# Strassen's seven block products in a float32 attention and mixture-of-experts kernel, ordered by a list scheduler at build time

## The chip, the cores and the metric

The kernel runs on one core of a Trainium2 chip. The core has a matrix engine (TensorE, "PE" in the profile, with its weight loads shown apart as "PEld"), a vector engine (VectorE, "DVE"), a scalar engine (ScalarE, "ACT"), GpSimd ("POOL") and SyncE ("SP"), whose queue issues all of this kernel's DMA transfers. Each engine runs its own instructions in order and waits on semaphores for the others. The metric is the device time of one execution in microseconds (us); less is better.

## What is computed

Inputs are q, k and v (8 batches, 8 heads, 576 tokens, 64 dims), a gain g_norm (64), the probabilities of four experts for each of the 4608 tokens, and the experts' weights w1 (4 x 512 x 1024) and w2 (4 x 1024 x 512). All is float32.

```python
kv = np.einsum('bhsd,bhse->bhde', k, v)
out = np.einsum('bhsd,bhde->bhse', q, kv)
rms = np.sqrt(np.mean(out * out, axis=-1, keepdims=True) + 1e-06)
x = (out / rms * g_norm)            # then (B,H,S,D) -> (B*S, H*D) = (4608, 512)
p = domain_probs / (domain_probs.sum(-1, keepdims=True) + 1e-09)
for e in range(E):
    h = np.maximum(x @ w1[e], 0.0)
    out += p[:, e:e + 1] * (h @ w2[e])
```

Every token goes through all four experts, so the two matrix products of the experts, 4608 x 512 x 1024 and 4608 x 1024 x 512 for each of four, are most of the arithmetic.

## The kernel before

Tokens go through the experts in nine chunks of 512. Chunk b < 8 holds the first 512 tokens of batch b, the ninth the 64 tokens that remain of every batch. All weights stay in SBUF, loaded once (`load_w1` and `load_w2`, L102 to L114). The loops run over chunks outermost, then experts, then eight slices of 128 hidden units (the list `slots`, L296).

`up` (L227, matmul L232) makes one slice of hidden units for the 512 tokens of a chunk: four matmuls, each with a weight block of 128 x 128 and 512 columns of x, added up in one PSUM bank; then ACT takes the bank through relu into SBUF (L237). `down` (L240, matmul L246) multiplies each of the chunk's four token blocks with the 512 columns of w2 for that slice, one matmul for each block; the four sums stay in four PSUM banks over the eight slices. After the eighth, `merge` (L253) takes each bank, times the token's probability for this expert, into an accumulator in SBUF on DVE (L257 and L259), and after the fourth expert `store` (L266) writes it out.

The attention of a batch consists of pieces (`attention`, L211): `key_values` makes k.T @ v for two heads (L151), `turn_q` transposes a block of queries (L170, copied on DVE at L172), `attend` multiplies (L181), squares on ACT (L186), sums on DVE (L188), takes the power on GpSimd (L189 and L193), and scales on DVE (L194); `turn_x` transposes the result (L207) and ACT writes it, times g, to the chunk's x (L209). Each batch has four blocks of 128 tokens and a remainder of 64.

The order of every engine is the order in which the code is written (`tc.manual_schedule`, L276). Batch 0's attention comes first and by itself. Then the slots follow: `up` of a slot, `down` of the slot before, and one piece of the next batch's attention after some of them (L308). SP's queue holds, in order, the loads of batch 0, the first expert's weights, g, the probabilities (L277 to L283), the next batches' loads and the stores.

Of the kernel before, what the change touches and what calls it, by code (L numbers as in the profile page):

```python
# [10 lines left out]
ALU = mybir.AluOpType  # L11
# [4 lines left out]

@with_exitstack
def kernel(
# [27 lines left out]
    KC = DM // P  # L46
    FCH = F // P
    NCH = B + 1
    KR = 6
    KP = S // KR  # L50
    EPS = 1e-6
    assert H * D == DM == NT and D == 64 and P == 128 and KC == NPAIR
# [3 lines left out]
    wpool = ctx.enter_context(tc.tile_pool(name="wpool", bufs=1))  # L56
    inpool = ctx.enter_context(tc.tile_pool(name="inpool", bufs=1))
    apool = ctx.enter_context(tc.tile_pool(name="apool", bufs=2))
    xpool = ctx.enter_context(tc.tile_pool(name="xpool", bufs=2))
    hpool = ctx.enter_context(tc.tile_pool(name="hpool", bufs=3))  # L60
    opool = ctx.enter_context(tc.tile_pool(name="opool", bufs=1))
    psum_a = ctx.enter_context(tc.tile_pool(name="psum_a", bufs=2, space=bass.MemoryType.PSUM))
    psum_h = ctx.enter_context(tc.tile_pool(name="psum_h", bufs=2, space=bass.MemoryType.PSUM))
    psum_o = ctx.enter_context(tc.tile_pool(name="psum_o", bufs=1, space=bass.MemoryType.PSUM))
# [4 lines left out]
    x_rem = const.tile([P, KC, NT], F32, name="x_rem")  # L69
    kv_bd = [const.tile([P, NPAIR, P], F32, name=f"kv_bd{i}") for i in range(2)]  # L70
    NBLK = NCH * NR
# [3 lines left out]
    w1_sb = [wpool.tile([P, KC, F], F32, name=f"w1_{e}") for e in range(E)]  # L75
    w2_sb = [wpool.tile([P, FCH, DM], F32, name=f"w2_{e}") for e in range(E)]

# [1 line left out]
    keys, values, queries, queries_rem = {}, {}, {}, {}  # L79

    def load_kv(b):
        for hp in range(NPAIR):
            hs = slice(2 * hp, 2 * hp + 2)
            for kept, src, tag in ((keys, k, "k"), (values, v, "v")):
                t = inpool.tile([KP, 2, KR, D], F32, tag=tag, bufs=2, name=f"{tag}{b}_{hp}")
                nc.sync.dma_start(
                    out=t[:].rearrange("p h j d -> p h (j d)"),
                    in_=src[b, hs].rearrange("h (p j) d -> p h (j d)", j=KR),
                )
                kept[b, hp] = t  # L90

    def load_q(b):
        t = inpool.tile([P, NR, H, D], F32, tag="q", name=f"q{b}")
        src = q[b, :, 0:NT, :].rearrange("h (p r) d -> p r h d", r=NR)
        for r in range(NR):
            nc.sync.dma_start(out=t[:, r], in_=src[:, r])  # L96
        queries[b] = t
        t = inpool.tile([REM, H, D], F32, tag="qr", name=f"qr{b}")
        nc.sync.dma_start(out=t[:], in_=q[b, :, NT:S, :].rearrange("h p d -> p h d"))  # L99
        queries_rem[b] = t  # L100

    def load_w1(e):  # L102
        n = 2 if e == 0 else 1
        for i in range(n):
            fs = slice(i * F // n, (i + 1) * F // n)
            nc.sync.dma_start(
                out=w1_sb[e][:, :, fs],
                in_=moe_w1[e][:, fs].rearrange("(kc p) f -> p kc f", p=P),
            )

    def load_w2(e):
        nc.sync.dma_start(
            out=w2_sb[e][:], in_=moe_w2[e].rearrange("(fc p) d -> p fc d", p=P)
        )  # L114

    def load_probs():
        by_batch = moe_domain_probs.rearrange("(b s) e -> s b e", s=S)
        nc.sync.dma_start(
            out=p_all[:, 0:B * NR, :].rearrange("p (b r) e -> p b (r e)", r=NR),
            in_=by_batch[0:NT].rearrange("(p r) b e -> p b (r e)", r=NR),  # L120
        )
        for bb in range(2):
            nc.sync.dma_start(
                out=p_all[bb * REM:(bb + 1) * REM, B * NR:NBLK, :],
                in_=by_batch[NT:S, bb::2, :],
            )

    def norm_probs():
        nc.vector.reduce_sum(out=tot[:], in_=p_all[:], axis=AX.X)
        nc.vector.tensor_scalar_add(out=tot[:], in0=tot[:], scalar1=1e-9)  # L130
        nc.vector.reciprocal(out=inv[:], in_=tot[:])
        nc.vector.tensor_tensor(
            out=p_all[:], in0=p_all[:],
            in1=inv[:].unsqueeze(2).to_broadcast([P, NBLK, E]), op=ALU.mult,
        )

# [1 line left out]
    kv_ps, xT, qT, x_tok = {}, {}, {}, {}  # L138

    def bank(name):  # L140
        return psum_a.tile([P, NT], F32, tag="a", name=name)

    def key_values(b, hp):
        """k.T @ v of two heads; after the last pair, all heads' as diagonal blocks."""
        if hp == 0:
            kv_ps[b] = bank(f"kv{b}")
        ps = kv_ps[b][:, 0:NPAIR * D].rearrange("p (a d) -> p a d", d=D)
        kt, vt = keys.pop((b, hp)), values.pop((b, hp))
        for r in range(2):
            for j in range(KR):  # L150
                nc.tensor.matmul(  # L151
                    ps[r * D:(r + 1) * D, hp, :], lhsT=kt[:, r, j, :], rhs=vt[:, r, j, :],
                    start=(j == 0), stop=(j == KR - 1),
                )
        if hp == NPAIR - 1:
            for r in range(2):
                rows = slice(r * D, (r + 1) * D)
                nc.vector.tensor_copy(out=kv_bd[b % 2][rows, :, rows], in_=ps[rows])  # L158

    def rows_of(r):  # L160
        return P if r < NR else REM

    def turn_q(b, r):
        """Queries of block r (the remainder for r == NR) with head dims on partitions."""
        n = rows_of(r)
        ps = bank(f"qT_ps{b}_{r}")[:, 0:NPAIR * n].rearrange("p (a t) -> p a t", t=n)
        for hp in range(NPAIR):
            hs = slice(2 * hp, 2 * hp + 2)
            src = queries[b][:, r, hs, :] if r < NR else queries_rem[b][:, hs, :]
            nc.tensor.transpose(ps[:, hp, :], src, ident[:n, :n])  # L170
        t = apool.tile([P, NPAIR, P], F32, tag="qT", name=f"qT{b}_{r}")
        nc.vector.tensor_copy(out=t[:, :, 0:n], in_=ps)  # L172
        qT[b, r] = t

    def attend(b, r):
        """q @ (k.T @ v) of the block, each head's row over its root mean square."""
        n = rows_of(r)
        raw = bank(f"raw{b}_{r}")
        t = qT.pop((b, r))
        for hp in range(NPAIR):  # L180
            nc.tensor.matmul(  # L181
                raw[0:n, hp * P:(hp + 1) * P], lhsT=t[:, hp, 0:n], rhs=kv_bd[b % 2][:, hp, :],
            )
        x = apool.tile([P, H, D], F32, tag="x", name=f"x{b}_{r}")
        rawh = raw[0:n, :].rearrange("p (h d) -> p h d", d=D)
        nc.scalar.activation(out=x[0:n], in_=rawh, func=ACT.Square)  # L186
        ss = apool.tile([P, H], F32, tag="ss", name=f"ss{b}_{r}")
        nc.vector.reduce_sum(out=ss[0:n], in_=x[0:n], axis=AX.X)  # L188
        nc.gpsimd.tensor_scalar(  # L189
            out=ss[0:n], in0=ss[0:n], scalar1=1.0 / D, scalar2=EPS, op0=ALU.mult, op1=ALU.add,  # L190
        )
        rt = apool.tile([P, H], F32, tag="rt", name=f"rt{b}_{r}")
        nc.gpsimd.tensor_tensor(out=rt[0:n], in0=ss[0:n], in1=mhalf[0:n], op=ALU.pow)  # L193
        nc.vector.tensor_tensor(  # L194
            out=x[0:n], in0=rawh, in1=rt[0:n].unsqueeze(2).to_broadcast([n, H, D]), op=ALU.mult,
        )
        x_tok[b, r] = x

    def turn_x(b, r):
        """The block with model dims on partitions, by g_norm."""  # L200
        n = rows_of(r)
        if r == 0:
            xT[b] = xpool.tile([P, KC, NT], F32, tag="xT", name=f"xT{b}")
        x = x_tok.pop((b, r))[0:n].rearrange("p h d -> p (h d)")
        ps = bank(f"xT_ps{b}_{r}")[:, 0:KC * n].rearrange("p (c t) -> p c t", t=n)
        for kc in range(KC):
            nc.tensor.transpose(ps[:, kc, :], x[:, kc * P:(kc + 1) * P], ident[:n, :n])  # L207
# [131 lines left out]
```

## Time and profile before

| What | Before |
|---|---|
| Time, median of 3 runs (lowest to highest) | 2158.01 us (2157.3 to 2158.16) |
| Span of the profiled execution | 2155.6 us |
| DMA, from and to DRAM | 45.16 MB read, 9.44 MB written |
| Mean granted TensorE clock over the span | 0.999 of full speed |

The span runs from the first to the last instruction of one profiled execution; the time has some work around it that the span leaves out. "Busy" is the time in which an engine executed instructions. A group of the profile shows line, engine, operation, output and inputs by their names in the program, shape and count, then busy time and the mean of one in ns, then the engine's idle time just before these instructions and what ended it. A float32 matmul leaves two records. The mean of one matmul record is the time from its start to its end, and these overlap from one to the next; the pace of the engine is read from the distance between starts.

### The profile page before, as it was taken

The page shows a single profiled execution, that of the slowest core. Times are in us where ns is not written, and L with a number is a line of the kernel's source. Part 1 is how long each engine was busy: PE and PEld are TensorE (multiplying, and loading weights), DVE is VectorE, ACT ScalarE, POOL GpSimd, SP SyncE. Part 2 cuts the span into 40 slices and gives each one's busy share as a digit, 9 for nine tenths or more (in the row PEclk, how much of TensorE's full clock was granted, in tenths as well). Part 3 has the DMA queues.
Part 4 walks back from the last instruction along what each step waited for, and adds up shares of the span by engine and source line. Part 5 has one row for each costly group of instructions (what it writes and reads, how often), then busy time and mean ns, then how long its engine had stood idle before and what let it go on. Part 6 is the DMA issues. An engine that isn't in the chain of part 4 may idle for free.

```text
span 2155.6 us, 13617 instructions
## 1 busy us (share of the span) xinstructions
PE 2118.0 (98%) x6016; PEld 990.4 (46%) x6016; DVE 197.1 (9%) x287; ACT 222.8 (10%) x369; POOL 73.9 (3%) x86
## 2 busy tenths in 40 slices
PE   4999999999999999999999999999999999999998
PEld 4444444444444444444444444444444444444443
DVE  1011000110011001110010001100111000000000
ACT  1011100110011000110011001110011000000000
POOL 1001000100000000000010000000000000000000
PEclk9999999999999999999999999999999999999999
DMA  6180003000300003000300020000200000000000
GB/s 167 30 270 0 0 0 86 0 0 0 82 5 0 0 12 75 0 0 0 86 0 0 0 71 15 0 1 5 60 0 1 20 0 0 0 20 0 0 0 20
DMA packets 64666, 55.47 MB, mean 26 GB/s; under 512 B 41056, under 2 KB 53344, under 8 KB 64608
## 3 DMA queue, kind: packets, MB, share of 16 engines
q1 hardware_dynamic: 64608, 54.61, 9.4%
q8 instruction: 47, 0.77, 0.2%
q14 instruction: 11, 0.09, 0.0%
HBM read 45.16 MB, written 9.44 MB: 25 GB/s over the span
## 4 chain that ended last, share of the span: by engine, by line
PE 98%; DMA 1%; SPq 0%; POOL 0%; DVE 0%; ACT 0%; issue 0%; ACTq 0%
PE h_ps L232 46%; PE o L246 46%; PE kv L151 2%; PE raw L181 2%; PE xT_ps L207 1%; PE qT_ps L170 1%; DMA gcol<-in_g_norm_dram 1%; POOL rt L193 0%; SPq L96 0%; DMA v<-in_v_dram 0%; DVE x L194 0%; DVE ss L188 0%; ACT x L186 0%; SPq L282 0%; SPq L99 0%
## 5 line engine op out<-in xcount | busy, mean ns | idle before, releaser
L246 PE MATMUL o<-w,h 128*128 128x512 f32 x2304 | 1035.6, 592 | 0.0
L232 PE MATMUL h_ps<-xT,w 128*128 128x512 f32 x2048 | 928.0, 596 | 0.0
L246 PEld LDWEIGHTS o<-w,h 128*128 128x128 f32 x2304 | 437.8, 190 | 551.0 <-issue 551.0
L232 PEld LDWEIGHTS h_ps<-xT,w 128*128 128x128 f32 x2048 | 379.3, 190 | 431.1 <-issue 428.2
L237 ACT ACTIVATE h<-h_ps 128x512 f32<-128x512 f32 x288 | 172.0, 597 | 1626.4 <-PE h_ps L232 1626.4
L259 DVE SCALAR_TENSOR_TENSOR acc<-o,p_all,acc 128x512 f32<-128x512 f32 x108 | 81.1, 751 | 808.1 <-PE o L246 799.4
L232 PE MATMUL h_ps<-x_rem,w 128*128 128x512 f32 x256 | 115.1, 592 | 0.0
L232 PEld LDWEIGHTS h_ps<-x_rem,w 128*128 128x128 f32 x256 | 48.6, 190 | 61.2 <-issue 61.2
L193 POOL TENSOR_TENSOR rt<-ss,mhalf 128x8 f32<-128x8 f32 (+1 forms) x40 | 65.4, 1635 | 3.3
L188 DVE TENSOR_REDUCE ss<-x 128x8 f32<-128x512 f32 (+1 forms) x40 | 27.4, 684 | 399.6 <-ACT x L186 399.6
L189 POOL TENSOR_SCALAR ss<-ss 128x8 f32<-128x8 f32 (+1 forms) x40 | 7.8, 196 | 1569.6 <-DVE ss L188 1569.6
L151 PEld LDWEIGHTS kv<-v,k 96*64 96x64 f32 x768 | 45.3, 148 | 28.7 <-issue 28.7
L151 PE MATMUL kv<-v,k 96*64 96x64 f32 x768 | 49.6, 237 | 7.3 <-DMA v<-in_v_dram 7.3
L181 PEld LDWEIGHTS raw<-kv_bd,qT 128*128 128x128 f32 (+1 forms) x320 | 44.2, 197 | 20.2 <-issue 19.0
L181 PE MATMUL raw<-kv_bd,qT 128*128 128x128 f32 (+1 forms) x320 | 46.9, 294 | 0.8 <-DVE qT L172 0.8
L158 DVE COPY kv_bd<-kv 64x256 f32<-64x256 f32 x16 | 6.8, 422 | 394.6 <-PE kv L151 394.5
L207 PE MATMUL xT_ps<-ident,x 128*128 128x128 f32 (+1 forms) x160 | 25.1, 283 | 17.1 <-DVE x L194 17.1
L186 ACT ACTIVATE x<-raw 128x512 f32<-128x512 f32 (+1 forms) x40 | 23.8, 596 | 151.2 <-PE raw L181 151.2
L257 DVE TENSOR_SCALAR acc<-o,p_all 128x512 f32<-128x512 f32 x36 | 27.0, 751 | 131.6 <-PE o L246 128.6
L172 DVE COPY qT<-qT_ps 128x512 f32<-128x512 f32 (+1 forms) x40 | 25.5, 637 | 137.0 <-PE qT_ps L170 137.0
L207 PEld LDWEIGHTS xT_ps<-ident,x 128*128 128x128 f32 (+1 forms) x160 | 19.6, 150 | 39.0 <-issue 19.3
L194 DVE TENSOR_TENSOR x<-raw,rt 128x512 f32<-128x512 f32 (+1 forms) x40 | 27.6, 690 | 81.4 <-POOL rt L193 81.4
(19 smaller groups left out, 75.1 us busy)
## 6 DMA issues: line engine op xcount, KB each, us to landing
w<-in_moe_w_dram SPq DMA_DIRECT2D x7, 2048.0 KB, 18.4
k<-in_k_dram SPq DMA_DIRECT2D x32, 288.0 KB, 3.4
v<-in_v_dram SPq DMA_DIRECT2D x32, 288.0 KB, 4.0
q<-in_q_dram SPq DMA_DIRECT2D x32, 256.0 KB, 5.3
out_dram<-acc SPq DMA_DIRECT2D x32, 256.0 KB, 4.4
w<-in_moe_w_dram SPq DMA_DIRECT2D x2, 1024.0 KB, 7.9
qr<-in_q_dram SPq DMA_DIRECT2D x8, 128.0 KB, 4.7
out_dram<-acc SPq DMA_DIRECT2D x8, 128.0 KB, 2.3
```

The costliest lines, as they stand in the source:

```text
L151: nc.tensor.matmul(ps[r * D:(r + 1) * D, hp, :], lhsT=kt[:, r, j, :], rhs=vt[:, r, j, :], start=(j == 0), stop=(j == KR - 1),)
L172: nc.vector.tensor_copy(out=t[:, :, 0:n], in_=ps)
L181: nc.tensor.matmul(raw[0:n, hp * P:(hp + 1) * P], lhsT=t[:, hp, 0:n], rhs=kv_bd[b % 2][:, hp, :],)
L188: nc.vector.reduce_sum(out=ss[0:n], in_=x[0:n], axis=AX.X)
L193: nc.gpsimd.tensor_tensor(out=rt[0:n], in0=ss[0:n], in1=mhalf[0:n], op=ALU.pow)
L194: nc.vector.tensor_tensor(out=x[0:n], in0=rawh, in1=rt[0:n].unsqueeze(2).to_broadcast([n, H, D]), op=ALU.mult,)
L207: nc.tensor.transpose(ps[:, kc, :], x[:, kc * P:(kc + 1) * P], ident[:n, :n])
L232: nc.tensor.matmul(ps[:], lhsT=w1_sb[e][:, kc, fc * P:(fc + 1) * P], rhs=src[:, kc, :], start=(kc == 0), stop=(kc == KC - 1),)
L237: nc.scalar.activation(out=h[:], in_=ps[:], func=ACT.Relu)
L246: nc.tensor.matmul(o_ps[r][:], lhsT=h[:, r * P:(r + 1) * P], rhs=w2_sb[e][:, fc, :], start=(fc == 0), stop=(fc == FCH - 1),)
L257: nc.vector.tensor_scalar_mul(out=acc[r][:], in0=o_ps[r][:], scalar1=prob)
L259: nc.vector.scalar_tensor_tensor(out=acc[r][:], in0=o_ps[r][:], scalar=prob, in1=acc[r][:], op0=ALU.mult, op1=ALU.add,)
```

## The change

The matrix products of the experts are divided into blocks of halves in each of the three dimensions, and each product of two 2 x 2 block matrices is made with seven block products and additions (Strassen's scheme in Winograd's form) in place of eight. `up` and `down` do this each for itself: one step s is one expert on one chunk of 512 tokens, 36 steps in all, with the experts outermost now.

For that, sums and differences of blocks are needed. Of each expert's w1 and w2, four blocks are loaded and four more formed (`weights_1`, `weights_2`); of each chunk's x, four are formed (`x_forms`). As the experts are outermost, each chunk's x comes back for every expert: all seven blocks are written to DRAM when they are first made, and read from there for experts 1 to 3 (`x_again`). In the same way a chunk's partial output is written to DRAM after experts 0 to 2 and read back before the next.

In `up`, the products go in the order 1, 2, 6, 5, 7, 4, 3, each for two halves i of the columns. A product is four float32 matmuls with 256 columns. Products 1, 6, 7 and 4 add up in one PSUM bank, 5 and 3 in another that product 2 has used; between them ACT copies the bank, or DVE adds a copy to it and ACT takes the relu. From the four blocks of h that result, four more are formed on DVE or GpSimd. `down` works the same way for two halves t of the tokens; each time that a bank holds a term of the output, DVE merges its 256 columns, times the probability, into the output block.

```diff
+    def up(s, e, views):
...
+        for j, m in enumerate(ORDER):
+            for i in range(2):
...
+                if m == 1:
+                    banks[i, 1] = Buf("ub", f"u1_{n}")
+                elif m in (2, 5):
+                    banks[i, 2] = Buf("ub", f"u2_{n}")
+                ps = banks[i, 1 if m in (1, 6, 7, 4) else 2]
+
+                def product(eng, m=m, i=i, ps=ps):
+                    for u in range(2):
+                        cols = slice((2 * i + u) * P, (2 * i + u + 1) * P)
+                        for kt in range(2):
+                            nc.tensor.matmul(
+                                ps.ap[:, u * HN:(u + 1) * HN],
+                                lhsT=two(w1f[e][m].ap[:])[:, kt, cols], rhs=views[m][1]()[:, kt, :],
+                                start=(m in (1, 2, 5) and u == 0 and kt == 0), stop=(kt == 1),
+                                skip_group_check=True,
+                            )
...
+                if m in (1, 6, 7):
...
+                if m == 2:
+                    total(unit(1), ps, banks[i, -1])
+                elif m == 7:
+                    total(unit(4), banks[i, 2], banks[i, -7])
+                elif m == 4:
+                    relu(unit(2), ps, key - 0.4)
+                elif m == 3:
+                    total(unit(21), ps, banks[i, -6])
...
+                    form(5, 21, 4, ALU.add)
+                    form(7, 1, 21, ALU.subtract)
+                    form(6, 5, 1, ALU.subtract)
+                    form(3, 2, 6, ALU.subtract)
...
+    def down(s, e, c):
...
+        for t in range(2):
+            banks = {}
+            for j, m in enumerate(ORDER):
+                key = base + (7 * t + j + 0.5) / 14
+                kind = "ab" if e and t else "db"
...
+                def product(eng, m=m, t=t, ps=ps):
+                    for kt in range(4):
+                        src = h[m, kt // 2].ap[:].rearrange("p (u t) -> p u t", u=2)
+                        nc.tensor.matmul(
+                            ps.ap[:, 0:HN], lhsT=src[:, kt % 2, t * P:(t + 1) * P],
+                            rhs=w2f[e][m].ap[:, kt * HN:(kt + 1) * HN],
+                            start=(m in (1, 2, 5) and kt == 0), stop=(kt == 3),
+                            skip_group_check=True,
+                        )
...
+                if m in (1, 2):
+                    merge(key, ps, t, 0)
+                elif m in (6, 3):
+                    merge(key, ps, t, 1)
+                elif m in (5, 7):
+                    merge(key, ps, 2 + t, 1)
+                elif m == 4:
+                    merge(key, ps, 2 + t, 0)
```

SBUF and PSUM are divided into numbered slots: 20 "big" tiles of 1024 columns (blocks of weights, x of expert 0's chunks), 46 "small" ones of 512 (h, x, sums, attention), and eight PSUM banks: four for `up` ("ub"), two for `down` ("db") and two ("ab") for the attention, which `down` uses too for experts 1 to 3.

```diff
+    BANKS = {"ub": 4, "db": 2, "ab": 2}
+    SLOTS = {"big": 20, "small": 46, "kv": 6, "kvbd": 8, "ss": 4, "rt": 4, **BANKS}
...
+    def either(n):
+        return {"DVE": 0.17 + 0.00108 * n, "POOL": 0.1 + 0.0025 * n}
```

No engine's order is written by hand any more. Every operation is added to a plan with a key (its due time, in steps), an assumed duration on each engine that can do it, and what it reads and writes. Down products of step s have keys between s + 1 and s + 2, those of the up products of step s + 1, so that both kinds share PE. The planner (`Plan.layout`) goes through time with these assumed durations: whenever an engine is free, it starts the first operation in order of keys whose inputs and slots are ready by then, looking ahead of the earliest one that is left by at most `REACH` steps (0.7 on PE, 0.9 on DVE, ACT and GpSimd, 1.0 on SP). An operation marked `either` goes to DVE or GpSimd, whichever is free first. The order that results is written out, and the real waits are put in from the tiles' reads and writes.

```diff
+                for op in pending:
+                    if op.key > reach:
+                        break
...
+                    when = ready(op, eng)
+                    if when is None:
+                        continue
+                    if when > t:
+                        heapq.heappush(wake, when)
+                        continue
+                    op.start, op.eng = t, eng
...
+    attention(0, -2.0, 1.3, 0.1)
+    weights_1(0, -0.9, 0.02)
+    x_views = {0: x_forms(0, -0.2, 0.02)}
+    weights_2(0, 0.0, 0.02)
+    norm_probs(0.1)
+    for e in range(E):
+        for c in range(NCH):
+            s = e * NCH + c
+            if e == 0 and c + 1 < B:
+                attention(c + 1, s - 0.1, 0.8, s + 0.5)
+            if e + 1 < E and c == NCH - 1:
+                weights_1(e + 1, s + 0.0, 0.12)
+                weights_2(e + 1, s + 1.0, 0.12)
+            if s + 1 < E * NCH:
+                if e == 0 and c + 1 < NCH:
+                    x_views[s + 1] = x_forms(c + 1, s + 0.75, 0.03)
+                else:
+                    x_views[s + 1] = x_again((c + 1) % NCH, s + 0.05, 0.13)
+            up(s, e, x_views.pop(s))
+            down(s, e, c)
+
+    order = plan.layout(slots)
```

The attention is the same arithmetic, in pieces by pair of heads now: for each of four pairs, the transposes of its queries for all four blocks, k.T @ v, the product, the norm (`scaled`), and the transposes of the result. Its matmuls are as many and as wide as before. The copies of transposed queries and of k.T @ v go to ACT instead of DVE. The remainder of 64 tokens comes later, keyed half a step into the step in which the next batch's attention runs (for batch 0, early in step 0). The two loads of g go first on SP's queue.

More of the change, by code (lines that the diff above doesn't have):

```diff
@@ L74 @@
     inv = const.tile([P, NBLK], F32, name="inv")
[L75 to L81, printed above, removed]
+    BANKS = {"ub": 4, "db": 2, "ab": 2}
+    SLOTS = {"big": 20, "small": 46, "kv": 6, "kvbd": 8, "ss": 4, "rt": 4, **BANKS}
+    SHAPE = {"big": 2 * NT, "small": NT, "kv": 2 * KR * D, "kvbd": P, "ss": H, "rt": H}
+    slots = {
+        kind: [
+            (psum if kind in BANKS else pool).tile(
+                [P, SHAPE.get(kind, NT)], F32, tag=f"{kind}{i}", name=f"{kind}{i}"
+            )
+            for i in range(n)
+        ]
+        for kind, n in SLOTS.items()
+    }
@@ new lines, with pe, dve, act @@
+    x_kept = {
+        (c, m): dram.tile([P, NT], F32, tag=f"x{c}_{m}", name=f"x{c}_{m}")
+        for c in range(NCH) for m in range(1, 8)
+    }
+    out_kept = {
+        (c, i): dram.tile([P, DM], F32, tag=f"o{c}_{i}", name=f"o{c}_{i}")
+        for c in range(NCH) for i in range(NR)
+    }
+    plan = Plan()
+    def pe(columns, passes=2):
+        return {"PE": passes * columns * 2.02 / 2400 + 0.003}
+    def dve(n):
+        return {"DVE": 0.17 + 0.00108 * n}
+    def act(n):
+        return {"ACT": 0.19 + 0.00088 * n}
@@ L160, in rows_of @@
[L160 to L207, printed above, removed]
-        dst = xT[b][:, :, r * P:(r + 1) * P] if r < NR else x_rem[:, :, b * REM:(b + 1) * REM]
-        nc.scalar.activation(out=dst, in_=ps, func=ACT.Copy, scale=gcol[:])
@@ L310 @@
-        down(*before)
+        for op in order:
+            op.fn(op.eng)
 _INS = ['q', 'k', 'v', 'g_norm', 'moe_domain_probs', 'moe_w1', 'moe_w2']
```

644 lines of the change are left out of this document (488 added, 156 removed).

## The prediction

> **What bounds the kernel now.** I read the page first (busy shares, the chain that ended last), then the busy time by windows, then the timeline.
>
> ```profile
> span 2155.6 us, 13617 instructions
> PE 2118.0 (98%) x6016; PEld 990.4 (46%) x6016; DVE 197.1 (9%) x287; ACT 222.8 (10%) x369; POOL 73.9 (3%) x86
> PE 98%; DMA 1%; SPq 0%; POOL 0%; DVE 0%; ACT 0%; issue 0%; ACTq 0%
> ```
>
> The span is TensorE: 98% busy, and the chain that ended last runs 98% through it. No other engine passes 10%. A busy PE need not be at its peak, so I look at its pace: is there a shape of work for which it does the same in less time?
>
> ```profile
> L246 PE MATMUL o<-w,h 128*128 128x512 f32 x2304 | 1035.6, 592 | 0.0
> L232 PE MATMUL h_ps<-xT,w 128*128 128x512 f32 x2048 | 928.0, 596 | 0.0
> L232 PE MATMUL h_ps<-x_rem,w 128*128 128x512 f32 x256 | 115.1, 592 | 0.0
> ...
> 329.75:565.20 235.45, 235.45 (x690) 110.07 (x689) 22.92 (x33) 25.31 (x42) 9.15 (x10) 1.00 0.08 20
> 1800.00:2000.00 200.00, 200.00 (x467) 88.54 (x466) 12.02 (x16) 17.44 (x30) 0.00 (x0) 1.00 0.02 6
> 2000.00:2155.60 155.60, 149.63 (x349) 65.93 (x347) 9.02 (x12) 12.54 (x21) 0.00 (x0) 0.99 0.03 7
> ```
>
> The columns of the windows are the stretch, its length, then busy time and count for PE, PEld, DVE, ACT and POOL, the granted clock, the DMA share and GB/s. The experts' matmuls are 2304 + 2048 + 256 = 4608 records (each float32 matmul leaves two). From 1800 to 2000 us nothing else runs: 467 records fill 200.00 us, **0.4283 us a record**, idle nothing, clock 1.00. So the experts hold 4608 x 0.4283 = 1973.5 us. The stretch from 329.75 to 565.20 is one whole chunk with a batch's attention in it: 512 expert records (219.3 us) and 235.45 - 219.3 = **16.2 us of attention**. After PE's last matmul (149.63 us into the last stretch) come 6.0 us of stores. Before the first expert matmul at 59.69 us lies the first batch's attention. Check: 59.7 + 1973.5 + 7 x 16.2 + 6.0 = 2152.6, against the span of 2155.6. Only fewer records, shorter records, or a shorter start can help.
>
> **Fewer columns.** In the changed code one expert on one chunk is 14 up products and 14 down products, each of four float32 matmuls of 256 columns: 28 x 4 x 2 = 224 records of 256 columns where there were 128 of 512. Over 36 steps that is 8064 records, with 7/8 of the columns. All turns on what a record of 256 columns takes, which the trace has not. It has the neighbours:
>
> ```profile
> 207.77 1.05 PE L181 MATMUL raw<-kv_bd,qT 128*128 128x128 f32 x8
> 208.66 0.59 PE L232 MATMUL h_ps<-xT,w 128*128 128x512 f32 x1
> 207.77 0.86 PEld L181 LDWEIGHTS raw<-kv_bd,qT 128*128 128x128 f32 x7 [0.24 <-issue]
> ```
>
> Eight records of 128 columns take 208.66 - 207.77 = 0.89 us, 0.111 each, their weight loads beside them (seven in 0.86 us, 0.123 each). Lower bound for 256 columns: half of 0.4283, 0.2141. Upper bound: twice 0.111, 0.2225. The straight line through both shapes gives 0.2168; I take **0.217**: 8064 x 0.217 = 1750 us (bounds 1727 and 1794), 224 us less than now. Weight loads double in number, but at 0.123 us they fit under 0.217.
>
> A rule speaks against this. The Trainium skill, "TensorE: Matmul & The Clock Gate", section "Back-to-back issue gap", says that in a stream of weight loads and matmuls both set the spacing, and gives about 81 ns for 128 columns against 56 for a matmul by itself. If those 25 ns were added to each halved record the estimate from that page would be 0.239 us, 1928 us in all and a span near 2104. The row above speaks against it: 0.111 is 4 ns above a quarter of 0.4283, not 25; no run here shows 256 columns.
>
> **What comes beside it.** Rows for the new work on the other engines:
>
> ```profile
> L237 ACT ACTIVATE h<-h_ps 128x512 f32<-128x512 f32 x288 | 172.0, 597 | 1626.4 <-PE h_ps L232 1626.4
> L259 DVE SCALAR_TENSOR_TENSOR acc<-o,p_all,acc 128x512 f32<-128x512 f32 x108 | 81.1, 751 | 808.1 <-PE o L246 799.4
> L194 DVE TENSOR_TENSOR x<-raw,rt 128x512 f32<-128x512 f32 x32 | 22.1, 692 | 65.3 <-POOL rt L193 65.3
> L172 DVE COPY qT<-qT_ps 128x512 f32<-128x512 f32 x32 | 22.1, 691 | 114.5 <-PE qT_ps L170 114.5
> L172 DVE COPY qT<-qT_ps 128x256 f32<-128x256 f32 x8 | 3.4, 423 | 22.5 <-PE qT_ps L170 22.5
> masks.py:199 POOL TENSOR_SCALAR_AFFINE_SELECT ident<-ident 128x128 f32<-128x128 f32 x1 | 0.3, 292 | 0.1
> ```
>
> Per step ACT gets 6 copies and 8 relus of 512 columns: 14 x 0.60 = 8.4 us. DVE gets 6 sums of a bank and a tile (0.69 each), 14 merges of 256 columns (0.751 less the 0.268 by which a copy shortens from 512 to 256: 0.48) and up to 8 forms of h (0.69): 4.1 + 6.7 + 5.5 = 16.3 us. A step's PE time is 224 x 0.217 = 48.6 us, so DVE is a third busy and ACT a sixth: as busy time all this costs nothing; if PE did not cover it, DVE alone would still be short of the span. The forms of x (36) and of the weights (32 of 1024 columns) add some 65 us over the whole. Forms may go to GpSimd; a two-input operation there has no row. Bounds: 0.29 us (a 128-column select) and, far off, a DVE-like 0.69 times several; I take four times the select, 1.2 us.
>
> PSUM banks are handed over often: M1 must be read before M6 is added to it, M6 before M7, M7 before M4, M5 (with M7's copy) before M3. That is four reads a column of products, 16 a step. One takes 0.60 (ACT) or 0.48 (DVE) and about 0.25 to be seen on either side. Up and down products of 8 x 0.217 = 1.74 us alternate, so a product of the other kind covers one; where none does, 0.8 us shows. Here I put nothing but a **10 us** allowance over 36 steps (bounds 0 and, below, the slower rival).
>
> ```profile
> 108.00:162.00 54.00, 54.00 (x183) 26.07 (x182) 6.61 (x10) 5.46 (x9) 1.83 (x2) 1.00 0.79 269
> q1 hardware_dynamic: 64608, 54.61, 9.4%
> out_dram<-acc SPq DMA_DIRECT2D x32, 256.0 KB, 4.4
> 10.60 4.35 SPq L96 DMA_DIRECT2D q<-in_q_dram  x4
> ```
>
> DRAM traffic: 63 stores and 189 reloads of x tiles, 108 stores and 108 reloads of partial outputs, 468 x 0.262 = 123 MB on top of 55 MB: some 92 GB/s over the new span, where 269 GB/s have run while PE stood at 54.00 of 54.00. A reload lands in about 4.4 us and is issued up to a step ahead. SP issues 15 such DMAs a step; even at the 1.09 us of the dearest (q, in pieces of 256 B) that is 16 of 48.6 us. What waits on SP behind a store's sum is the next reload, and it has tens of us. Cost: nothing, if the tiles' slots allow the lead.
>
> **Start and end.** Now the first attention goes block by block:
>
> ```profile
> 37.97 1.12 PE L207 MATMUL xT_ps<-ident,x 128*128 128x128 f32 x4 [2.83 <-DVE x L194]
> 44.93 1.11 PE L207 MATMUL xT_ps<-ident,x 128*128 128x128 f32 x4 [3.29 <-DVE x L194]
> 51.89 1.12 PE L207 MATMUL xT_ps<-ident,x 128*128 128x128 f32 x4 [3.52 <-DVE x L194]
> 59.69 1.22 PE L232 MATMUL h_ps<-xT,w 128*128 128x512 f32 x1
> ACT xT L209 <- DMA gcol<-in_g_norm_dram: 12.0, 1, 12.0
> ```
>
> Each block takes 6.96 us. After the change there are four head pairs of about that chain, the remainder is put off into the first step, and g is loaded first, so the 12.0 us for it go. Four times 7 after about 5 us of loading, and 3 us of forms: 36 us; then the first up has no down beside it to cover its hand-offs, 4 us more: **40** (bounds 30 and 60). The remainder of batch 0 costs 3, batches 1 to 7 the same 16.2 each, 113 (their PE work is unchanged in columns). The last down stands alone: 4. Drain 6.
>
> Sum: 40 + 1750 + 113 + 3 + 10 + 4 + 6 = 1926 us of span. Before, the median of 2158.0 stands 2.4 above the profiled span; so **1928 us**, 10.7% less.
>
> **Rivals.**
> *The weight loads show.* If loads and matmuls get in each other's way as at 128 columns, the record is 0.2225 and the time 1928 + 44 = 1972; by the page's 25 ns, named above, more. For it: the loads double. Against: PEld is 46% busy now.
> *DVE and GpSimd block each other.* Forms of h become ready in pairs, so one goes to each engine. If one held the other up, a merge behind it would come late: some 3 forms a step on GpSimd x 1.2 us x 36 = 126 us if nothing covers it, 2054. The Trainium skill, "SBUF — State Buffer", section "Who interferes with whom", says that a VectorE instruction with two SBUF inputs and a GpSimd one that reads SBUF exclude each other for their whole length; the forms are of that kind, and no run here shows a pair. Against its full price: forms of h are due a fifth of a step later.
> *Reloads come late.* The 46 small tiles hold h, x and sums together; if a slot were free only after its reload should have begun, a landing of 4.4 us shows in each of 27 reload steps: 119 us, 2047. Against: 269 GB/s beside a full PE.
> *Slower: hand-offs bare.* If PE's order puts products of one bank next to each other, each of 16 x 36 = 576 hand-offs stops PE for up to 0.8 us: 1928 + 461 = 2389. It decides from 0.40 us on average (230 / 576), half of them uncovered. For it: in each column M4 follows M7 directly. Against: the other kind of product, 1.74 us, can stand between.
> *It doesn't do what it says*: as many PE columns as before, so about 2158.
>
> **Chances.** Forecast (1885 to about 1960) 0.63; weight loads 0.10; blocking 0.13; late reloads 0.05; bare hand-offs 0.07; no saving 0.02. A measurement of this kernel tells 0.2% (4 us) from no change. Faster: 0.63 + 0.10 + 0.13 + 0.05 = 0.91; same 0.01; slower 0.07 + 0.01 = 0.08. The range, 1885 (0.2141 a record and a start of 30) to 2025, holds the forecast, the weight loads and most of the blocking: about 0.8.
>
> **What would show it.** Right: 8064 expert records, one every 0.217 us in stretches without attention; PE idle under 1% after the first step; first expert product near 30 to 40 us. Wrong: records further apart with no wait between (weight loads); PE waiting for DVE or ACT at the bank's next product (hand-offs), with DVE idle behind GpSimd (blocking); PE or DVE waiting for a DMA (reloads).

## The result and the profile after

The changed kernel takes **1884.2 us** (median of 4 runs, 1882.7 to 1884.8) where the kernel before takes 2158.0 us: a ratio of 0.873 (95% interval 0.8717 to 0.8742), 12.7% less time. The forecast was 1928 with a range from 1885, so the time lies just under the range's lower end. What was removed and what bounds the kernel had been read rightly; most terms of the sum were too large, the attention's and those for hand-offs above all.

First the page of the changed kernel, and from its list of groups by shape the experts' matmuls:

```profile
span 1883.0 us, 23222 instructions
PE 1858.1 (99%) x9472; PEld 1629.1 (87%) x9472; DVE 624.3 (33%) x978; ACT 390.9 (21%) x697; POOL 376.4 (20%) x277
PE 97%; SPq 2%; DMA 1%; issue 0%; DVE 0%
```

```profile
L624 PE MATMUL ub<-small,big 128*128 128x256 f32 x3600 | 852.4, 380 | 0.0
...
L749 PE MATMUL db<-big,small 128*128 128x256 f32 x2520 | 596.0, 380 | 0.0
...
L749 PE MATMUL ab<-big,small 128*128 128x256 f32 x1512 | 356.2, 379 | 0.0
...
L624 PE MATMUL ub<-big,big 128*128 128x256 f32 x384 | 91.7, 383 | 0.0
...
L624 PE MATMUL ub<-x_rem,big 128*128 128x256 f32 x48 | 11.3, 379 | 0.0
```

The span is still TensorE, now 99% busy, and the records are 3600 + 2520 + 1512 + 384 + 48 = 8064, as counted. DVE is a third busy and DMA moves 178.81 MB, also as worked out. Then the stretches:

```profile
241.41:303.21 61.80, 61.80 (x402) 53.75 (x401) 22.74 (x36) 18.75 (x38) 17.92 (x17) 1.00 0.36 105
```

```profile
1500.00:1700.00 200.00, 200.00 (x928) 176.08 (x927) 61.29 (x99) 36.04 (x59) 23.24 (x16) 1.00 0.23 79
```

In 200 us without attention 928 records are counted, 0.2155 us each; but such a count takes in records that only reach into the window, as the forecast's count of 467 did. From start to start the pace is a little slower: between 1500.20 and 1648.69 us stand 688 records, **0.2158 us** each, and in the kernel before 336 records take 144.20 us from 1802.70 on, 0.4292 each and not 0.4283. (The forecast took 0.217.) The stretch from 241.41 to 303.21 is one step of expert 0 with a batch's attention in it: 61.80 - 224 x 0.2158 = **13.5 us of attention**, where the forecast kept 16.2. By starts, that 16.2 is itself only 235.45 - 512 x 0.4292 = 15.7. PE's own waits, over the whole execution, longest first:

```profile
PE ab L491 <- DVE small L409: 10.4, 4, 4.1
PE ab L448 <- DMA small<-in_q_dram: 5.6, 1, 5.6
PE ab L463 <- DMA kv<-in_v_dram: 1.5, 1, 1.5
...
PE ab L545 <- DVE small L409: 0.5, 1, 0.5
```

None of them belongs to an up or down product (L624, L749), and none lies after 130 us. No hand-over of an expert's bank, no reload and no form of h ever stops PE. The start and the end, in the order of time:

```profile
39.47 2.51 PE L624 MATMUL ub<-big,big 128*128 128x256 f32 x8
...
1854.16 12.38 PE L749 MATMUL db<-big,small 128*128 128x256 f32 x56
1866.38 12.25 PE L749 MATMUL ab<-big,small 128*128 128x256 f32 x56
```

The first expert product begins at 39.47 us (59.69 before), and the last down, alone, runs through without a wait until 1866.38 + 12.25 = 1878.6; 4.4 us of stores follow.

So the difference to the forecast's span of 1926 can be laid out by its own terms:

| Term | Forecast, us | Measured, us |
|---|---|---|
| Start until the first expert product | 36 | 39.5 |
| 8064 records | 1750 | 8064 x 0.2158 = 1740.2 |
| Attention of batches 1 to 7 | 113 | 7 x 13.5 = 94.5 |
| Remainder of batch 0; bare hand-offs of the first up and the last down; allowance for waits | 3 + 4 + 4 + 10 | 4.4 (what is left) |
| Stores at the end | 6 | 4.4 |
| Span | 1926 | 1883.0 |

The forecast's start of 40 held the first up's 4; here they stand in the fourth row. Of the 4.4 us in that row, 1.8 are PE's two waits behind 45 us, 1.3 at L491 and 0.5 at L545; both belong to the attention, so next to nothing is left for hand-offs.

### The profile page after: what moved, and what is told of

The parts are those of the page before. It is cut to its first block, busy times and chain, and to the rows that moved or that the text cites. A ratio compares the mean times of both kernels' runs of the same rounds, so it can differ in the third digit from the quotient of the medians.

```text
span 1883.0 us, 23222 instructions
## 1 busy us (share of the span) xinstructions
PE 1858.1 (99%) x9472; PEld 1629.1 (87%) x9472; DVE 624.3 (33%) x978; ACT 390.9 (21%) x697; POOL 376.4 (20%) x277
## 2 busy tenths in 40 slices
DMA packets 142074, 178.81 MB, mean 95 GB/s; under 512 B 49424, under 2 KB 76816, under 8 KB 141968
## 4 chain that ended last, share of the span: by engine, by line
PE 97%; SPq 2%; DMA 1%; issue 0%; DVE 0%
PE ub L624 46%; PE db L749 29%; PE ab L749 17%; SPq L282 1%; PE ab L481 1%; PE ab L463 1%; PE ab L491 1%; PE ab L448 1%; PE ab L530 0%; DMA big<-in_moe_w_dram 0%; DMA small<-in_q_dram 0%; SPq L298 0%; PE ab L545 0%; PE ab L515 0%; DVE small L409 0%
## 5 line engine op out<-in xcount | busy, mean ns | idle before, releaser
L624 PE MATMUL ub<-small,big 128*128 128x256 f32 x3600 | 852.4, 380 | 0.0
L624 PEld LDWEIGHTS ub<-small,big 128*128 128x128 f32 x3600 | 681.5, 190 | 93.3 <-issue 0.9
L749 PE MATMUL db<-big,small 128*128 128x256 f32 x2520 | 596.0, 380 | 0.0
L749 PEld LDWEIGHTS db<-big,small 128*128 128x128 f32 x2520 | 475.3, 190 | 64.2 <-issue 0.6
L276 POOL TENSOR_TENSOR small<-small,small 128x512 f32<-128x512 f32 x145 | 210.0, 1456 | 1071.9 <-ACT small L640 1066.3
L749 PE MATMUL ab<-big,small 128*128 128x256 f32 x1512 | 356.2, 379 | 0.0
L749 PEld LDWEIGHTS ab<-big,small 128*128 128x128 f32 x1512 | 287.3, 190 | 39.1
L655 ACT ACTIVATE small<-ub 128x512 f32<-128x512 f32 x216 | 128.8, 597 | 681.4 <-PE ub L624 671.7
L276 DVE TENSOR_TENSOR small<-ub,small 128x512 f32<-128x512 f32 x216 | 149.4, 692 | 270.3 <-PE ub L624 139.3
L276 DVE TENSOR_TENSOR small<-small,small 128x512 f32<-128x512 f32 x143 | 160.6, 1123 | 4.6 <-ACT small L640 2.5
L276 POOL TENSOR_TENSOR big<-big,big 128x1024 f32<-128x1024 f32 x26 | 61.1, 2352 | 189.8 <-PE ub L624 105.0
L624 PE MATMUL ub<-big,big 128*128 128x256 f32 x384 | 91.7, 383 | 0.0
L624 PEld LDWEIGHTS ub<-big,big 128*128 128x128 f32 x384 | 71.7, 192 | 9.4 <-issue 0.2
L640 ACT ACTIVATE small<-ub 128x512 f32<-128x512 f32 x72 | 43.0, 597 | 152.1 <-PE ub L624 152.1
```

Source lines behind the costliest of these rows:

```text
L276: lambda eng: adder(eng).tensor_tensor(out=out_(), in0=a(), in1=b(), op=op),
L624: nc.tensor.matmul(ps.ap[:, u * HN:(u + 1) * HN], lhsT=two(w1f[e][m].ap[:])[:, kt, cols], rhs=views[m][1]()[:, kt, :], start=(m in (1, 2, ...
L640: lambda eng: nc.scalar.activation(out=b.ap[:], in_=src.ap[:], func=ACT.Relu),
L655: lambda eng, to=banks[i, -m], ps=ps: nc.scalar.activation(out=to.ap[:], in_=ps.ap[:], func=ACT.Copy),
L749: nc.tensor.matmul(ps.ap[:, 0:HN], lhsT=src[:, kt % 2, t * P:(t + 1) * P], rhs=w2f[e][m].ap[:, kt * HN:(kt + 1) * HN], start=(m in (1, 2, ...
```

## The experiments

The theory after the result: the forecast's mechanism is right, and its sum was 43 us too high: the record, the attention's cost on PE, the allowances for hand-offs and the stores were too large, and only the start was 3.5 us too short. Rivals: that the records come nearer to each other only in the new order; that the attention got cheaper through its new order and not through something in it; that hand-offs, GpSimd or reloads do cost time that something else hides.

### What a record of 256 columns costs (e1)

In the kernel before, each matmul of `up` and `down` is cut into two:

```diff
-        for kc in range(KC):
-            nc.tensor.matmul(
-                ps[:], lhsT=w1_sb[e][:, kc, fc * P:(fc + 1) * P], rhs=src[:, kc, :],
-                start=(kc == 0), stop=(kc == KC - 1),
-            )
+        for u in range(2):
+            us = slice(u * 256, (u + 1) * 256)
+            for kc in range(KC):
+                nc.tensor.matmul(
+                    ps[:, us], lhsT=w1_sb[e][:, kc, fc * P:(fc + 1) * P], rhs=src[:, kc, us],
+                    start=(kc == 0 and u == 0), stop=(kc == KC - 1), skip_group_check=True,
+                )
...
+                    o_ps[r][:, us], lhsT=h[:, r * P:(r + 1) * P], rhs=w2_sb[e][:, fc, us],
```

> The kernel before with every matmul of up and down cut into two of 256 columns: 9216 expert records instead of 4608, the same columns in all, no Strassen. It prices the record of 256 columns by itself. Theory (the record takes 0.2155 us, as 928 in 200 us of the changed kernel show): 9216 x 0.2155 = 1986 us against 1973.5, so about 2158 + 12.5 = 2170 us. The forecast's line through two shapes (0.2168): 1998, about 2182. Rival, the weight loads show as at 128 columns (0.2225): 2050, about 2235. By the page's 25 ns a record (0.239): about 2387.

Measured: 2169.6 us (ratio 1.0056, 1.0039 to 1.0072), 11.5 us more. The same window as before:

```profile
1800.00:2000.00 200.00, 200.00 (x928) 176.08 (x927) 12.02 (x16) 17.32 (x29) 0.00 (x0) 1.00 0.02 6
```

The same 928 records in 200 us, and 0.2158 us by starts (672 records in 145.04 us), without any Strassen: the pace belongs to the shape. Half of 0.4292 is 0.2146, so halving a matmul costs 1.2 ns a record, and over 9216 records that is the whole difference (11.5 us / 9216 = 1.25 ns). The forecast's line through 128 and 512 columns gave 2.7, its upper bound 8.4. PEld is busy 176.08 of 200 us and still does not show. The 25 ns that the Trainium skill ("TensorE: Matmul & The Clock Gate", "Back-to-back issue gap") suggests for a stream of pairs at 128 columns are not there at 256; the measurement decides.

### Why the attention is cheaper (e2, e4)

In `key_values`, the matmuls of two heads write to PSUM partitions 0 to 63 and 64 to 127. Before, the six of one head came first and then those of the other; the changed kernel alternates. e2 puts the new order into the old kernel (shown), e4 the old order into the new kernel:

```diff
-        for r in range(2):
-            for j in range(KR):
+        for j in range(KR):
+            for r in range(2):
```

> The kernel before with the two loops of key_values exchanged, so that matmuls of the two heads alternate between the lower and the upper 64 PSUM partitions. Theory (the alternation shortens a group of 24 records from 1.36 to 0.85 us): 0.51 x 4 x 7 = 14 us less for batches 1 to 7, perhaps 2 more at the start: about 2143 us. Rival (the attention became cheaper through the order of its pieces by pairs of heads): no change, 2158 us, groups still 1.36 us apart.

> The changed kernel with the loops of key_values back in the old order (one head's six matmuls after the other's). Theory (of the 2.7 us that a batch's attention became cheaper, 2.0 come from the alternation): 1884 + 14 to 16 = 1898 to 1900 us, with a group of 24 records 1.36 us long. Rival (the saving comes from elsewhere, or PE had slack there): 1884 us.

Measured: e2 2143.1 us (0.9935, 0.992 to 0.9949), 14.9 less than before; e4 1901.3 us (0.8813, 0.8799 to 0.8826), 17.2 more than the changed kernel. One group of 24 records and the matmul behind it, first in e2 and then in e4:

```profile
92.22 0.92 PE L151 MATMUL kv<-v,k 96*64 96x64 f32 x24
93.07 3.70 PE L232 MATMUL h_ps<-xT,w 128*128 128x512 f32 x8
```

```profile
274.42 1.43 PE L463 MATMUL ab<-kv,kv 96*64 96x64 f32 x24
275.78 1.99 PE L624 MATMUL ub<-big,big 128*128 128x256 f32 x8
```

From start to start a group takes 0.85 us when it alternates and 1.36 us when it does not: 35 ns a record against 57. Four groups a batch make 0.51 x 4 = 2.0 of the 2.2 us between 15.7 and 13.5, and 0.51 x 28 = 14.3 us of the whole; both kernels answer to the same edit. Of the 2.9 us by which e4 loses more, 1.5 are in the start, where its first expert product comes at 40.98 us instead of 39.47; the rest is open. The loops' order was in the diff, and the forecast did not weigh it. The Trainium skill, "TensorEngine Tiling (Array Packing)", "Key Properties", says that tiles in different places of the array load weights and multiply in parallel; the trace agrees with that, though no run tells the loads from the multiplying. The other 0.2 us a batch were not tried by themselves.

### Loading g first (e3)

```diff
+        for i in range(P // D):
+            nc.sync.dma_start(out=gcol[i * D:(i + 1) * D, :], in_=g_norm.unsqueeze(1))
         load_kv(0)
         load_q(0)
         load_w1(0)
         load_w2(0)
-        for i in range(P // D):
-            nc.sync.dma_start(out=gcol[i * D:(i + 1) * D, :], in_=g_norm.unsqueeze(1))
```

> The kernel before with the two loads of g moved ahead of all others on SP's queue. Theory (ACT's 12.0 us wait for g was on the path to the first expert matmul and nothing else is late behind it): first expert matmul near 48 us, 2158 - 11 = about 2147 us. Rival (k and v now land later, or the weights are not there at 48 us): less than 5 us gained, 2153 or more.

Measured: 2153.5 us (0.9978, 0.9969 to 0.9987), 4.6 us less: the rival. The first expert matmul comes at 55.28 us instead of 59.69. Of PE's waits in the first 60 us, those that changed, in the kernel before and in e3:

```profile
PE kv L151 <- DMA v<-in_v_dram: 7.3, 2, 5.0
PE qT_ps L170 <- ACT xT L209: 6.4, 1, 6.4
```

```profile
PE kv L151 <- DMA v<-in_v_dram: 9.8, 3, 6.8
```

ACT's 12.0 us wait for g had cost PE only 6.4 us, which are gone in e3, and k and v, which now come behind g, take 2.5 of them back. The forecast's start let all 12.0 go.

### The hand-offs of banks (e7, e8)

e7 takes PE's look-ahead out of the planner (the first pair of lines); e8 also moves all up products of a step ahead of its down products (the others, with the loads and stores of the output moved alike).

```diff
-    REACH = {"PE": 0.7, "DVE": 0.9, "ACT": 0.9, "POOL": 0.9, "SP": 1.0}
+    REACH = {"PE": 0.02, "DVE": 0.9, "ACT": 0.9, "POOL": 0.9, "SP": 1.0}
...
-                key = s + (2 * j + i) / 14
+                key = s + (2 * j + i) / 28
-        base = s + 1.0
+        base = s + 0.5
-                key = base + (7 * t + j + 0.5) / 14
+                key = base + (7 * t + j + 0.5) / 28
```

> The changed kernel with PE's look-ahead in the planner cut from 0.7 to 0.02 steps: PE takes its products in the order of keys, up and down in turn. It is the control of the next one. Theory (a product of the other kind, 1.72 us, covers each hand-off of about 0.85 us): from expert 1 on the steps stay at 224 x 0.2155 = 48.3 us with PE full, 27 of them 1303 us. In expert 0 the attention's chains are no longer filled with other products, so some tens of us are lost there. Rival (the look-ahead does the hiding, not the other kind): 50 us and more a step from expert 1 on.

> As e7, but the keys put all up products of a step ahead of all its down products, so that none of the other kind stands between. Theory (hand-offs cost what they are bare): in down M4 follows M7 directly, twice a step, 0.85 us each, and the first forms of h are not ready when up ends, 2 to 4 us: 52 to 54 us a step from expert 1 on in place of 48.3. The forecast's slower rival (all 16 hand-offs bare at 0.8 us): 61 us a step. If hand-offs cost nothing even so: 48.3.

Measured, one run each: e7 1901.4 us, e8 2046.7 us. The same stretch in e7 and in e8, and PE's waits in it in e8:

```profile
1000.00:1300.00 300.00, 300.00 (x1392) 264.09 (x1391) 95.12 (x152) 53.16 (x87) 44.26 (x29) 1.00 0.25 86
```

```profile
1000.00:1300.00 300.00, 280.07 (x1262) 240.50 (x1261) 98.20 (x144) 46.35 (x78) 47.88 (x26) 0.99 0.23 79
```

```profile
PE db L749 <- DVE small L276: 13.6, 6, 3.5
PE db L749 <- DVE small L704: 3.5, 6, 0.6
PE ab L749 <- DVE small L704: 2.9, 5, 0.6
```

In turn, e7 keeps 1392 records in 300 us, 48.3 us a step. Of the 17 us that it loses, 15 are lost before 500 us (PE has 3017 records by then, 69 fewer than in the changed kernel; its first product comes at 48.92 us), and 1.5 in the last down, where no other kind stands beside it. Apart, e8 does 1262, or 300 x 224 / 1262 = 53.2 us a step (52.8 from 500 to 1850 us). Two hand-offs a step are bare (M4 after M7 in down); the waits list shows 0.58 us for each, but it counts from the end of a record, which reaches 0.16 us past the next start. By starts, in e8:

```profile
1029.58 8.80 PE L749 MATMUL ab<-big,small 128*128 128x256 f32 x40
1038.95 3.72 PE L749 MATMUL ab<-big,small 128*128 128x256 f32 x16 [0.58 <-DVE small L704]
```

Forty records take 9.37 us instead of 40 x 0.2158 = 8.63: a bare hand-off costs 0.74 us, close to the forecast's 0.8. At the start of down PE waits for h's forms (L276), 13.6 / 6 = 2.3 us a step, and runs slower behind a long wait: after one of 3.45 us the next 20 records took 6.27 us instead of 4.48, with a granted clock of 0.50 from 1021 to 1023 us. So the slower rival's mechanism exists. Standing apart costs 145 us in all, 2046.7 - 1901.4, of which 72 hand-offs at 0.74 make 53; the rest is the wait for the forms and what follows it. Alternating with a product of the other kind hides all of it. The forecast named that cover and then still put 18 us for hand-offs in the first up, in the last down and as an allowance.

### DVE and GpSimd side by side (e5, e6)

All the forms (sums of two blocks in SBUF) on one engine, DVE in e5 (shown), GpSimd in e6 (where the entry for POOL stays alone):

```diff
     def either(n):
-        return {"DVE": 0.17 + 0.00108 * n, "POOL": 0.1 + 0.0025 * n}
+        return {"DVE": 0.17 + 0.00108 * n}
```

> The changed kernel with all sums of blocks (forms of x, h and weights) on DVE, none on GpSimd. Theory (DVE's forms take 1.12 us in place of 0.69 only because GpSimd's run beside them; PE waits for neither): forms of 512 columns back at 0.69 us, those of 1024 near 1.23, time unchanged, 1884 us within 3. Rival (the blocking makes merges late and costs PE time that only the records' overlap hides): several us less, 1875 or under. Rival (DVE alone becomes late): 1895 or more.

> The changed kernel with all these sums on GpSimd, none on DVE. Theory: GpSimd's 512-column form falls from 1.456 to about 1.27 us (the shortest that it now takes), since DVE's remaining operations have one SBUF input; 288 x 1.27 + 32 x 2.4 + 80 = about 520 us busy of 1884, time unchanged within 3 us after the start, perhaps 2 to 5 us more in the start, where the four forms of x and w1 follow each other. Rival (a form of 1.3 us in place of 0.7 shows on the chain to h): 10 us and more.

Measured: e5 1885.2 us (0.8729, 0.8715 to 0.8744), e6 1892.7 us (0.8769, 0.8756 to 0.8782). The forms of h in the changed kernel, by mean ns, and then alone in e5 and in e6 (least, median and most ns):

```profile
L276 POOL TENSOR_TENSOR small<-small,small 128x512 f32<-128x512 f32 x145 | 210.0, 1456 | 1071.9 <-ACT small L640 1066.3
...
L276 DVE TENSOR_TENSOR small<-small,small 128x512 f32<-128x512 f32 x143 | 160.6, 1123 | 4.6 <-ACT small L640 2.5
```

```profile
L276 DVE TENSOR_TENSOR small<-small,small x288: 678/681/693, 78.0 to 1859.5; 128x512 f32<-128x512 f32 x144
```

```profile
L276 POOL TENSOR_TENSOR small<-small,small x288: 1256/1267/1287, 83.5 to 1866.6; 128x512 f32<-128x512 f32 x144
```

Alone, a form takes 0.68 us on DVE and 1.27 on GpSimd; together 1.12 and 1.46. So the two do hold each other up, as the Trainium skill ("SBUF — State Buffer", "Who interferes with whom") says of operations with two SBUF inputs, and DVE loses 143 x (1.123 - 0.681) = 63 us of its own time. The changed kernel loses none that can be measured: without it, in e5, the time is the same, and PE had no wait to give back.

e6 is 8.6 us slower, not the 2 to 5 expected. In its first 130 us PE is busy 103.0 us against 109.4, and behind that it is full. These 6.4 us are two longer waits for the attention's norm: 6.19 us instead of 4.14 at L491, where GpSimd gets to the norm's power only after four forms of weights, and 4.84 instead of 0.53 at L545:

```profile
50.01 7.39 DVE L305 TENSOR_SCALAR tot<-tot 128x36 f32<-128x36 f32 x1
50.41 6.94 POOL L276 TENSOR_TENSOR big<-big,big 128x1024 f32<-128x1024 f32 x3
...
59.49 0.66 PE L545 MATMUL ab<-ident,small 64*128 64x64 f32 x4 [4.84 <-DVE small L409]
```

L305 adds a constant to one small tile. It takes 0.18 us in e5, 1.04 in the changed kernel and 7.39 here, for as long as three forms follow each other on GpSimd, and what PE needs stands behind it on DVE. So it is the start and not the chain to h, and in it the blocking does cost the kernel something, 4.3 us by this row. It strikes an operation with a single tensor input, which the expectation had left out. The last 2.2 of the 8.6 us are open.

### Reloads (e9)

```diff
-    REACH = {"PE": 0.7, "DVE": 0.9, "ACT": 0.9, "POOL": 0.9, "SP": 1.0}
+    REACH = {"PE": 0.7, "DVE": 0.9, "ACT": 0.9, "POOL": 0.9, "SP": 0.1}
...
-                    x_views[s + 1] = x_again((c + 1) % NCH, s + 0.05, 0.13)
+                    x_views[s + 1] = x_again((c + 1) % NCH, s + 1.1, 0.14)
```

> The changed kernel with SP's look-ahead in the planner cut from 1.0 to 0.1 steps and the reloads of x keyed at the step that uses them, up to 0.1 steps behind its first product (before: almost a whole step ahead). Theory (PE takes down products while it waits for x): from expert 1 on still 48.3 us a step. The forecast's rival (a landing of 4.4 us shows in each step): 52.7 us a step, 119 us in all. The start is that of e11.

Measured: 1881.9 us in one run; from 500 to 1850 us PE is busy 1350.00 of 1350.00. Counted from the trace, the changed kernel issues its reloads about two steps ahead of the product that uses them, e9 mostly 0.2 to 0.7 steps, 10 to 34 us. With a landing of 4.4 us they are still in time. So a step and a half of lead less costs nothing, and the rival with late reloads falls for the changed kernel; that PE would take down products while it waits for x was not put to the test.

### The start (e10, e11, e12)

What is left is the start. e10 gives the first batch's attention idle banks of `up` and `down` (the lines with banks), e11 cuts SP's look-ahead as e9 does (the lines with REACH), e12 does both.

```diff
-    REACH = {"PE": 0.7, "DVE": 0.9, "ACT": 0.9, "POOL": 0.9, "SP": 1.0}
+    REACH = {"PE": 0.7, "DVE": 0.9, "ACT": 0.9, "POOL": 0.9, "SP": 0.1}
...
-            bank = Buf("ab", f"qT{n}")
+            bank = Buf("ab" if b else "db", f"qT{n}")
...
-            bank = Buf("ab", f"kv{n}")
+            bank = Buf("ab" if b else "db", f"kv{n}")
...
-            bank = Buf("ab", f"xT{n}")
+            bank = Buf("ab" if b else "ub", f"xT{n}")
```

> The changed kernel with the first batch's attention on six idle PSUM banks of up and down besides its own two. Theory A (the start is held by two banks that four head pairs share): first expert product at about 32 us in place of 39.5, 1884 - 7 = 1877 us. Theory B (it is held by SP's order: the first weights and the second batch's queries go ahead of the fourth pair's k and v): no gain, 1882 to 1885.

> The changed kernel with SP's look-ahead cut from 1.0 to 0.1 steps, and nothing else: the loads go nearly in the order of their keys, the fourth pair's k and v ahead of the weights. Theory B: first expert product at 30 to 34 us, 6 to 9 us less, 1875 to 1878 us, and no wait for reloads later. Theory A: 1882 to 1885. Rival: what is loaded later than now (weights, second batch) is late in its turn, 1884 or more.

> e10 and e11 together. If both hold the start one after the other: 2 to 4 us below e11, about 1873 us. If only SP's order does: as e11.

Measured: e10 1882.9 us (0.8726, 0.8711 to 0.874), e11 1882.2 us (0.8719, 0.8706 to 0.8732; four runs from 1878.4 to 1882.9), e12 **1873.8 us** (0.8683, 0.867 to 0.8696). SP's queue in the changed kernel, then in e12:

```profile
11.06 3.16 SPq L282 DMA_DIRECT2D big<-in_moe_w_dram  x4
14.34 0.40 SPq L282 DMA_DIRECT2D kv<-in_k_dram  x1
```

```profile
12.13 0.54 SPq L282 DMA_DIRECT2D kv<-in_k_dram  x1
12.71 0.45 SPq L282 DMA_DIRECT2D kv<-in_v_dram  x1
13.21 3.58 SPq L282 DMA_DIRECT2D big<-in_moe_w_dram  x4
...
22.90 4.55 SPq L282 DMA_DIRECT2D small<-in_q_dram  x3
```

The changed kernel sends 2 MB of weights ahead of the fourth pair's k, since the planner found no free slot for it yet (six for k and v, three pairs hold them) and looked on. Neither theory holds alone: more banks bring 1.2 us, the loads' order 1.9, both together 10.4. The first expert product comes at 37.84, 33.01 and 28.66 us in the profiles of e10, e11 and e12, against 39.47. The profiled run of e11 is its fastest, 1878.4 us at a mean granted clock of 0.999; its other three stand at 0.994. That the start is held by whichever of the two is left fits these numbers, but the clock moved with them, and no run parts the two. e12 beats both kernels.

## Why the forecast was too high

- **What bounds the kernel** and **fewer columns**: right. 8064 records, PE full, no record waits for its weights. The record was a little mis-sized: 0.2158, where the line gave 0.2168 and 0.217 was taken; 10 us. The 0.4283 and the 0.2141 of the lower bound come from a count in a window; by starts they are 0.4292 and 0.2146.
- **"batches 1 to 7 the same 16.2 each, 113 (their PE work is unchanged in columns)"**: this is the step that failed. The columns are the same, but two loops were exchanged, and with them 24 records take 0.85 us in place of 1.36, so that the attention takes 13.5 us a batch, 94.5 in place of 113. These 18.5 us are the largest term of the miss: 14.3 come from the loops, as e2 and e4 show in both kernels, 3.5 from the 16.2, which should have been 15.7, and the rest was not traced.
- **Hand-offs**: the cover by alternation was argued rightly and then not believed: 10 + 4 + 4 us were put on top, and with the remainder of batch 0 all of this came to 4.4 us instead of 21. It is the second term of the miss, 16.6 us. e8 shows the price without the cover, 0.74 us each.
- **What comes beside it** on ACT, DVE, GpSimd and DMA: right, at no cost to PE. A merge took 0.48 us as worked out; GpSimd's form 1.27 alone, 1.2 forecast.
- **Start**: 36 forecast, 39.5 measured, and the reasons were off on both sides: g's wait was worth 4.6 us, not 12.0 (e3), and the loads' order and two banks hold the first product (e12), as far as the granted clock does not.
- **The range**: its low end moved the record and the start (0.2141 and 30). That gives 1928 - 23 - 10 = 1895; to come to 1885 the allowance of 10 must go as well. The attention and the other hand-offs stayed where they were. Had these been given their own lower ends, the true time would have been well inside.
- **Rivals**: weight loads, late reloads and "doesn't do what it says" did not come. The blocking of DVE and GpSimd did come, at 63 us of DVE's time and none of the kernel's that shows (its price in the forecast, 3 x 1.2 x 36, is 130 and not 126); bare hand-offs come only if up and down are pulled apart, or in a last down in strict order (e7).

## What to carry to other kernels

When an engine is 98% busy at its full pace, work out the new time from counted records and the pace of that very shape, read from start to start, and look at every matmul loop in the diff, also at those whose columns do not change: the order of two loops was worth 15 us in one kernel and 17 in the other. A wait that is covered by argument should be costed at nothing in the sum, and its price kept for the range, with a low end for each term. Strassen's extra sums cost nothing here because two independent streams of products alternate on PE; without that, 4 us a step were lost (e8).

## What the runs showed of the hardware

- A float32 matmul of 256 columns leaves records 0.2158 us apart, 1.2 ns more than half of one with 512 (e1), with its weight load of 0.19 us beside it.
- An addition on DVE that takes 0.18 us by itself (e5) took 7.39 while three sums of two tiles ran on GpSimd one behind the other (e6).
- Matmuls of 64 columns that alternate between the two halves of PSUM's partitions run at 35 ns a record against 57 (e2, e4).
- In the start the granted clock (third number from the end in these windows of the changed kernel) falls to half while PE has little to do:

```profile
30.00:35.00 5.00, 3.02 (x26) 2.54 (x24) 4.04 (x4) 1.23 (x4) 0.00 (x0) 0.50 0.91 257
35.00:40.00 5.00, 2.29 (x10) 2.20 (x11) 1.04 (x2) 0.97 (x2) 3.43 (x4) 0.50 0.70 146
40.00:45.00 5.00, 5.00 (x27) 3.87 (x26) 3.27 (x3) 2.05 (x5) 0.89 (x1) 0.93 1.11 255
```

  The one run of e11 with a mean clock of 0.999 took 1878.4 us, the three at 0.994 took 1881.9 to 1882.9; e12, whose first products come earlier, stood at 0.999 in all four runs. The Trainium skill ("TensorE: Matmul & The Clock Gate", section "What's actually happening" of Part 1) names too little activity of the array as the cause; the three windows agree, and no run here separates it from other causes. The kernel before does not fit so simply: from 30 to 35 us its PE is busy 0.97 of 5 us and the row reads 1.00, as it does from 25 to 30 us, where eight records of 128 columns took 1.92 us instead of 1.05. Its mean clocks from 0.987 to 0.999 also go with times from 2156.5 to 2159.6 us in no order, so the row alone does not give the time.
